# Loading W_down and wo at the end of a decode kernel: one queue for wo, and W_down split over partitions 96 + 11 + 11 + 10

## The chip, the cores and the metric

The kernel runs on one core of a Trainium2 chip. The metric is the device time of one execution in microseconds (us). The core has five engines with instruction streams of their own: TensorE (PE, matmuls, with its weight loads listed apart as PEld), VectorE (DVE), ScalarE (ACT), GpSimd (POOL) and SyncE (SP). SP and ACT can issue DMAs; 16 DMA engines carry them out, between HBM and the on-chip memory of 128 partitions.

## The reference

It is one step of decoding, of a gated mix of two branches for 4 tokens x of width 512:

```python
g = sigmoid((x * gate_w).sum(-1, keepdims=True))
a = attention(x @ wq, last 4096 keys and values of the caches) @ wo   # 32 heads on 8 KV heads
b = (relu(x @ W_gate) * (x @ W_up)) @ W_down                          # F = 1792
return g * a + (1 - g) * b
```

All data are bf16. wq is 512x4096, wo 4096x512, W_gate and W_up 512x1792, W_down 1792x512. Keys and values of the window are 4 tokens x 8 heads x 4096 x 128 each, so that the kernel reads 81 MB, of which 64 MiB are keys and values.

## The kernel before, in words

**Sets.** Attention is done in 8 sets (a token and half of its heads each). Set s loads 4 MB of keys into `Ksb` and 4 MB of values into `Vsb`; both have two halves, used in turn. PE transposes the keys (L353), ACT and DVE copy them back (L358, L360), PE makes the scores (L374), DVE adds the mask and takes the maximum (L384), ACT takes the exponential (L404), DVE transposes the probabilities (L414) and PE multiplies them with the values (L422, the function `values`).

**Order of the transfers.** Apart from x, gate_w and one piece of wo, all loads are issued by SP, one after the other, and SP waits in order: a load of keys waits for the scores of two sets before (L218), a load of values for the product of two sets before (L222). After the last keys come W_gate and W_up into the first half of `Ksb` (L231, L233), the values of the last set (L222), then W_down into the first half of `Vsb` (L236), which waits for `PV` of set 6, the last reader of that half, and then wo into `Wbig` (L241, L244), which waits for nothing but stands behind W_down's wait on SP.

**W_down and wo in memory.** Each is laid out with 128 partitions: a partition holds a contiguous piece of HBM, 14 tiles of 512 for W_down (14 KB) and 32 tiles of 512 for wo (32 KB). W_down is one DMA of 128 rows of 14 KB. wo comes in six pieces along the row: tiles 0 to 2 in a DMA that ACT issues (L499, `WOE`), tiles 3 to 15, 16 to 25 and 26 to 29 in three DMAs by SP (L241, `WO`), and tiles 30 and 31 in two, one for each half of the columns (L244, `WOL`).

**The end.** After the last set's maximum and exponential PE combines the heads of the first half (L441), makes gate and up (L458), waits for the last values, does `values(7)` (L422) and `combine(1)` (L441, L444), which yields `oq`. Then PE adds all of W_down's and wo's products into one accumulator (L508, the helper `product`): 28 matmuls with W_down, 6 with tiles 0 to 2 of wo, 26, 20 and 8 with the pieces of `WO`, and 2 for each half of the columns of `WOL`. As soon as a half of the columns is done, DVE (L525) or ACT (L526) copies it, and SP sends the result out (L547).

**Engine programs.** The class `Program` holds one list of operations per engine. `P.dma` gives a transfer a semaphore of its own that counts to 16 when it has landed; a wait is for a named event, and PE waits on the constant that the event has in `P.events`. An operation waits only for what its list of events says, and each engine works its list in order.

Of the kernel before, what the change touches and what calls it, by code (L numbers as in the profile page):

```python
# [19 lines left out]
NSET = 8  # L20
NFT = FF // 128
# [5 lines left out]
NTR = 2  # L27
NPAIR = 2
NFILL = 8
WO_EARLY = 3  # L30
WO_CUTS = (3, 16, 26, 30)
ACT_TAKES = (1, 3, 4, 6, 7)


# [105 lines left out]
def bass_gated_mix__sliding_block_cached__glu_gated_reglu__decode_kernel(  # L140
# [13 lines left out]
    with ExitStack() as ctx:  # L154
        def sb(name, shape, dt):
            return ctx.enter_context(nc.sbuf_tensor(name, shape, dt))

        Ksb = sb("Ksb", [128, 2, 16384], BF16)
        Vsb = sb("Vsb", [128, 2, 16384], BF16)
        Wbig = sb("Wbig", [128, 16384], BF16)  # L160
# [44 lines left out]
        Wo3 = Wbig[:, :].rearrange("p (i w) -> p i w", w=512)  # L205

        P = Program()
# [13 lines left out]
        def load_v(s):  # L221
            P.dma("sp", lambda e: e.dma_start(Vsb[:, s % 2, :], heads(A_v_cache, s)), ("V", s),  # L222
                  [("PV", s - 2)] if s >= 1 else [], sem=loop_sem("V", s))
# [4 lines left out]
        for s in range(1, NSET):  # L228
# [4 lines left out]
        P.dma("sp", lambda e: e.dma_start(Ksb[:, 0, 4 * FF:8 * FF], B_W_up.rearrange("(p t) f -> p (t f)", p=128)),  # L233
              ("WU",), [("SC", NSET - 2, NPAIR - 1)])
        load_v(NSET - 1)
        P.dma("sp", lambda e: e.dma_start(Vsb[:, 0, 0:NFT * 512], B_W_down.rearrange("(p i) w -> p (i w)", p=128)),  # L236
              ("WD",), [("PV", NSET - 2)])
        wo_src = A_wo.rearrange("(p i) w -> p (i w)", p=128)
        for k in range(len(WO_CUTS) - 1):
            lo, hi = 512 * WO_CUTS[k], 512 * WO_CUTS[k + 1]  # L240
            P.dma("sp", lambda e, lo=lo, hi=hi: e.dma_start(Wbig[:, lo:hi], wo_src[:, lo:hi]), ("WO", k))  # L241
        wo_src3 = A_wo.rearrange("(p i) w -> p i w", p=128)
        for u in range(2):
            P.dma("sp", lambda e, u=u: e.dma_start(Wo3[:, WO_CUTS[-1]:32, 256 * u:256 * u + 256],  # L244
                                                   wo_src3[:, WO_CUTS[-1]:32, 256 * u:256 * u + 256]), ("WOL", u))

# [170 lines left out]
        def values(s):  # L417
            par = s % 2
            for blk in range(64):
                g = blk % 4  # L420
                w = [("PTT", s), ("V", s), ("OSB", s - 1)] if blk == 0 else []
                P.op("pe", lambda e, g=g, blk=blk: e.matmul(  # L422
                    OB[32 * g:32 * g + 32, 0:256], pT[:, par, 32 * blk:32 * blk + 32],
                    Vsb[:, par, 256 * blk:256 * blk + 256],
                    start=(blk < 4), stop=(blk >= 60), tile_position=(0, 32 * g)),
                    ("PV", s) if blk == 63 else None, w)
            if s < 0:
                P.op("act", lambda e: e.copy(idle[:, 1:2], onesf[:, 0:1]),
                     ("OSB", s), [("ONESF",)], sem="va")
            else:  # L430
                P.op("act", lambda e: e.copy(osb[:, s, :], OB[:, 0:256]), ("OSB", s), [("PV", s)], sem="va")  # L431
# [22 lines left out]
        def gateup():  # L454
            for t in range(4):
                for which, W in ((0, Wg), (1, Wu)):
                    for g in range(4):
                        P.op("pe", lambda e, which=which, W=W, t=t, g=g: e.matmul(  # L458
                            TRT[32 * g:32 * g + 32, 512 * which:512 * which + FQ], xT[:, t, :], W[:, t, FQ * g:FQ * g + FQ],
                            start=(t == 0), stop=(t == 3), tile_position=(0, 32 * g)),  # L460
                            ("GU", which) if (t == 3 and g == 3) else None,
                            [("WG",), ("WU",)] + fills[-NTR:])
            G0 = TRT[:, 0:FQ]
            G1 = TRT[:, 512:512 + FQ]
            P.op("act", lambda e: e.activation(hrelu[:, :], G0, ACTF.Relu),
                 ("H0",), [("GU", 0)])
            P.op("dve", lambda e: e.tensor_tensor(
                hrow[:, :].rearrange("p (i c) -> p c i", i=NFT), G1.rearrange("p (c i) -> p c i", i=NFT),
                hrelu[:, :].rearrange("p (c i) -> p c i", i=NFT), ALU.mult), ("H1",), [("H0",), ("GU", 1)])
            P.op("dve", lambda e: e.transpose(hcol[:, :], hrow[:, :]), ("H2",), [("H1",)])  # L470
            P.op("dve", lambda e: e.tensor_tensor(
                hT[:, :].rearrange("p (i b) -> p i b", b=4),
                hcol[:, :].rearrange("p (i b) -> p i b", b=32)[:, :, 0:4],
                gsb[:, 4:8].rearrange("p (o b) -> p o b", o=1).to_broadcast([128, NFT, 4]), ALU.mult),
                ("H",), [("H2",), ("G",)], sem="vd")
# [19 lines left out]
        turn(NSET - 1)  # L495
        combine(0)
        gateup()
        early = 0
        P.dma("act", lambda e: e.dma_start(Wbig[:, 0:512 * WO_EARLY], wo_src[:, 0:512 * WO_EARLY]), ("WOE", 0), [], sem="wos")  # L499
        early = 16  # L500
        P.events[("WOE",)] = ("wos", early, None, 0)
        values(NSET - 1)
        combine(1)
        AB = SCT[:, 0:512]
        oq3 = oq[:, :].rearrange("p (b i) -> p b i", b=4)

        def product(stat, mov, u, start, stop, name, waits):
            P.op("pe", lambda e: e.matmul(AB[32 * u:32 * u + 4, 0:256], stat, mov[:, 256 * u:256 * u + 256],  # L508
                                          start=start, stop=stop, tile_position=(0, 32 * u)), name, waits)

        for i in range(NFT):
            for u in range(2):
                product(hT[:, 4 * i:4 * i + 4], Wd[:, i, :], u, i == 0, False, None,
                        [("WD",), ("H",), ("SCC", NSET - 1, 1)])
        for i in range(WO_EARLY):
            for u in range(2):
                product(oq3[:, :, i], Wo3[:, i, :], u, False, False, None, [("WOE",), ("OQ", 0), ("OQ", 1)])
        for k in range(len(WO_CUTS) - 1):
            for i in range(WO_CUTS[k], WO_CUTS[k + 1]):
                for u in range(2):  # L520
                    product(oq3[:, :, i], Wo3[:, i, :], u, False, False, None, [("WO", k)])
        for u in range(2):
            for i in range(WO_CUTS[-1], 32):
                product(oq3[:, :, i], Wo3[:, i, :], u, False, i == 31, ("ACC", u) if i == 31 else None, [("WOL", u)])
# [68 lines left out]
```

## Time and profile before

| | us |
|---|---|
| median of 3 runs | 196.21 |
| lowest and highest of these | 196.20 to 196.37 |
| the profiled execution's own time | 196.32 |
| its span, from the first to the last instruction | 195.1 |

The profiled execution lies 0.11 us above the median, and 1.2 us of its time lie outside its span. The profile lists each engine's busy time, the share of the 16 DMA engines that is busy in a stretch of time (1.00 is all 16), the chain of work that ended last, and groups of instructions by line. In a row of the timeline the columns are start, length, engine, line, operation, tiles, how many instructions were merged, and in brackets how long the engine was idle before and what released it.

### The profile page before, as it was taken

How to read it: one execution, taken by the hardware profiler on the slowest of the kernel's cores; microseconds unless marked ns; L12 is line 12 of the kernel's file. 1: busy time of each engine (PE TensorE's matmuls, PEld its weight loads, DVE VectorE, ACT ScalarE, POOL GpSimd, SP SyncE). 2: the span in 40 equal slices, each digit the busy share in tenths (PEclk: the TensorE clock that was granted, in tenths of full speed). 3: DMA queues.
4: the chain of work that ended last, by engine and by line, in shares of the span. 5: the costliest groups of instructions: out<-in, count | busy, mean ns of one | idle time of the engine just before them, and what ended most of it. 6: DMA issues, size and time to landing. Idle time of an engine off the chain costs nothing.

```text
span 195.1 us, 3497 instructions
## 1 busy us (share of the span) xinstructions
PE 129.0 (66%) x1578; PEld 101.0 (52%) x1578; DVE 73.8 (38%) x95; ACT 66.4 (34%) x77; POOL 11.6 (6%) x43
## 2 busy tenths in 40 slices
PE   0136398788669638861987298729964996732974
PEld 0112386576457427641965195519643974612752
DVE  0200054268239315820492039302931293280010
ACT  2005035465264453424243524352445244420000
POOL 8820000000000000000000000000000000000000
PEclk9999579999999999999799969975998599996699
DMA  6999999999999999999999999999999999999992
GB/s 216 437 437 437 437 437 433 430 433 430 430 433 443 437 437 430 430 430 430 432 430 432 430 430 430 430 430 430 430 430 430 430 401 432 456 430 391 418 408 73
DMA packets 4025, 81.11 MB, mean 416 GB/s; under 512 B 425, under 2 KB 946, under 8 KB 1202
## 3 DMA queue, kind: packets, MB, share of 16 engines
q1 hardware_dynamic: 3864, 80.61, 96.8%
q10 hardware_dynamic: 154, 0.40, 0.5%
q8 instruction: 5, 0.08, 0.2%
q14 instruction: 2, 0.02, 0.0%
HBM read 81.01 MB, written 0.00 MB: 415 GB/s over the span
## 4 chain that ended last, share of the span: by engine, by line
DMA 60%; PE 20%; DVE 14%; ACT 3%; issue 1%; SPq 1%
DMA Ksb<-in_A_k_cache_dram 48%; PE TRT L353 13%; DMA Wbig<-in_A_wo_dram 12%; DVE Ksb L360 7%; DVE pT L414 5%; PE SCT L374 3%; DVE sc L384 3%; ACT Ksb L358 3%; PE OB L422 2%; PE SCT L508 1%; SPq L241 0%; PE FB L391 0%; SPq L541 0%; ACT outr L526 0%; SPq L236 0%
## 5 line engine op out<-in xcount | busy, mean ns | idle before, releaser
L353 PE MATMUL TRT<-identw,Ksb 128*128 128x128 f32 x512 | 74.9, 306 | 27.1 <-DMA Ksb<-in_A_k_cache_dram 18.8
L353 PEld LDWEIGHTS TRT<-identw,Ksb 128*128 128x128 f32 x512 | 65.7, 158 | 37.3 <-DMA Ksb<-in_A_k_cache_dram 20.0
L358 ACT COPY Ksb<-TRT 128x1024 f32<-128x1024 f32 x40 | 40.5, 1012 | 59.6 <-PE TRT L353 59.5
L360 DVE COPY Ksb<-TRT 128x1024 f32<-128x1024 f32 x24 | 29.4, 1223 | 41.3 <-PE TRT L353 41.3
L422 PE MATMUL OB<-Vsb,pT 128*32 128x256 bf16 x576 | 18.9, 288 | 6.8 <-DMA Vsb<-in_A_v_cache_dram 6.8
L374 PE MATMUL SCT<-Ksb,qS 128*32 128x512 bf16 x256 | 16.9, 381 | 8.8 <-ACT Ksb L358 8.8
L422 PEld LDWEIGHTS OB<-Vsb,pT 128*32 128x32 bf16 x576 | 16.4, 102 | 9.7 <-issue 7.2
L384 DVE CUSTOM_DVE_ANT_0 sc<-SCT,mask,mx 128x1024 bf16<-128x1024 f32 x8 | 10.3, 1285 | 26.8 <-PE SCT L374 26.8
L404 ACT ACTIVATE sc<-sc,negmax 128x2048 bf16<-128x2048 bf16 x8 | 16.0, 2002 | 10.8 <-DVE negmax L396 10.8
L414 DVE STREAM_TRANSPOSE pT<-sc 128x2048 bf16<-128x2048 bf16 x8 | 18.4, 2302 | 2.2 <-ACT sc L404 2.2
L374 PEld LDWEIGHTS SCT<-Ksb,qS 128*32 128x32 bf16 x256 | 5.2, 94 | 15.7 <-ACT Ksb L358 11.4
L431 ACT COPY osb<-OB 128x256 f32<-128x256 f32 x8 | 3.0, 372 | 30.4 <-PE OB L422 30.4
L384 DVE CUSTOM_DVE_ANT_0 sc<-SCT,mask 128x1024 bf16<-128x1024 f32 x8 | 9.8, 1225 | 2.2 <-PE SCT L374 2.2
L341 POOL COPY qS<-qW 128x64 bf16<-128x64 bf16 x8 | 1.8, 237 | 112.6 <-PE SCT L374 104.5
L391 PE MATMUL FB<-identw,mx 128*128 128x128 f32 x18 | 4.4, 324 | 5.7 <-issue 5.7
L396 DVE CUSTOM_DVE_ANT_0 mrow<-FB,qmask 128x128 f32<-128x128 f32 x8 | 2.3, 291 | 12.8 <-PE FB L391 12.8
L391 PEld LDWEIGHTS FB<-identw,mx 128*128 128x128 f32 x18 | 2.7, 187 | 7.6 <-issue 7.6
L293 PE MATMUL FB<-identw,xw 5*128 5x5 f32 x4 | 0.6, 263 | 8.5 <-POOL m L268 8.5
L508 PE MATMUL SCT<-Wbig,oq 128*4 128x256 bf16 x64 | 4.4, 273 | 1.8 <-DMA Wbig<-in_A_wo_dram 1.8
L311 PE MATMUL SCT<-Vsb,xT 128*32 128x512 bf16 x32 | 3.6, 631 | 2.9 <-DMA Vsb<-in_A_wq_dram 2.9
L293 PEld LDWEIGHTS FB<-identw,xw 5*128 5x128 f32 x4 | 0.6, 206 | 8.5 <-DVE xw L287 8.5
L441 PE MATMUL TRT<-osb,Wsel 128*64 128x128 f32 x32 | 4.3, 292 | 0.5 <-ACT osb L431 0.5
(61 smaller groups left out, 41.7 us busy)
## 6 DMA issues: line engine op xcount, KB each, us to landing
Ksb<-in_A_k_cache_dram SPq DMA_DIRECT2D x8, 4096.0 KB, 25.0
Vsb<-in_A_v_cache_dram SPq DMA_DIRECT2D x8, 4096.0 KB, 32.9
Vsb<-in_A_wq_dram SPq DMA_DIRECT2D x1, 4096.0 KB, 12.3
Ksb<-in_B_W_gate_dram SPq DMA_DIRECT2D x1, 1792.0 KB, 18.9
Ksb<-in_B_W_up_dram SPq DMA_DIRECT2D x1, 1792.0 KB, 22.8
Vsb<-in_B_W_down_dram SPq DMA_DIRECT2D x1, 1792.0 KB, 16.9
Wbig<-in_A_wo_dram SPq DMA_DIRECT2D x1, 1664.0 KB, 20.5
Wbig<-in_A_wo_dram SPq DMA_DIRECT2D x1, 1280.0 KB, 23.1
```

Source lines behind the costliest of these rows:

```text
L311: P.op("pe", lambda e, half=half, t=t, g=g, col=col: e.matmul(SCT[32 * g:32 * g + 32, 512 * half:512 * half + 512], xT[:, t, :], Wq3[:, t, ...
L353: P.op("pe", lambda e, bk=bk, cc=cc, c=c: e.transpose(bk[:, cc * 128:(cc + 1) * 128], Kw[:, s % 2, c * 128:(c + 1) * 128], identw[:, :]), ...
L358: P.op("act", lambda e: e.copy(dst, bk), ("KTC", s, i), [("KT", s, i)], sem="va")
L360: P.op("dve", lambda e: e.tensor_copy(dst, bk), ("KTC", s, i), [("KT", s, i)], sem="vd")
L374: P.op("pe", lambda e, a=a, o=o, hb=hb, bank=bank: e.matmul(SCT[32 * a:32 * a + 32, 512 * hb:512 * hb + 512], qS[:, s % 2, o, :], k4[:, 16 ...
L384: P.op("dve", lambda e: e.tensor_tensor_reduce(sc[:, s % 2, pair * 1024:(pair + 1) * 1024], SCT[:, :], mask[:, :], 1.0, mx[:, s % 2, 0:1] ...
L391: P.op("pe", lambda e: e.matmul(FB[:, 384:512], mx[:, par, 1:2].to_broadcast([128, 128]), identw[:, :], start=True, stop=True), ("MT", s), ...
L404: P.op("act", lambda e: e.activation(sc[:, par, :], sc[:, par, :], ACTF.Exp, bias=negmax[:, par:par + 1], scale=SCALE, accum_out=rowsum[:, ...
L414: P.op("dve", lambda e: e.transpose(pT[:, par, :], sc[:, par, :]), ("PTT", s), [("EXP", s), ("PV", s - 2) if s >= 1 else None], sem="vd")
L422: P.op("pe", lambda e, g=g, blk=blk: e.matmul(OB[32 * g:32 * g + 32, 0:256], pT[:, par, 32 * blk:32 * blk + 32], Vsb[:, par, 256 * blk:256 ...
L441: P.op("pe", lambda e, k=k, lo=lo: e.matmul(CB[r, 0:128], Wsel[:, lo:lo + 64], ov[:, half, :, 32 * k:32 * k + 32], start=(k == 0), stop=(k ...
L508: P.op("pe", lambda e: e.matmul(AB[32 * u:32 * u + 4, 0:256], stat, mov[:, 256 * u:256 * u + 256], start=start, stop=stop, tile_position=( ...
```

## The change

All of wo is now issued by SP: the piece that ACT issued is gone, and SP's first piece of wo holds tiles 0 to 15 instead of 3 to 15. W_down, 128 rows before in one DMA, now comes in four: the first carries partitions 0 to 95, the other three carry partitions 96, 99, ... 126 (11 rows), 97, 100, ... 127 (11 rows) and 98, 101, ... 125 (10 rows). All four count on one semaphore, and PE waits until it has 64. The products with tiles 0 to 2 of wo now stand behind the landing of the first piece.

```diff
-WO_EARLY = 3
-WO_CUTS = (3, 16, 26, 30)
+WO_CUTS = (0, 16, 26, 30)
...
-        P.dma("sp", lambda e: e.dma_start(Vsb[:, 0, 0:NFT * 512], B_W_down.rearrange("(p i) w -> p (i w)", p=128)),
-              ("WD",), [("PV", NSET - 2)])
+        wd_src = B_W_down.rearrange("(p i) w -> p (i w)", p=128)
+        wd_parts = [slice(0, 96)] + [slice(96 + a, 96 + a + 3 * n - 2, 3) for a, n in ((0, 11), (1, 11), (2, 10))]
+        for k, part in enumerate(wd_parts):
+            P.dma("sp", lambda e, part=part: e.dma_start(Vsb[part, 0, 0:NFT * 512], wd_src[part, :]),
+                  ("WD", k), [("PV", NSET - 2)], sem="wd")
+        P.events[("WD",)] = ("wd", 16 * len(wd_parts), None, 0)
...
-        early = 0
-        P.dma("act", lambda e: e.dma_start(Wbig[:, 0:512 * WO_EARLY], wo_src[:, 0:512 * WO_EARLY]), ("WOE", 0), [], sem="wos")
-        early = 16
-        P.events[("WOE",)] = ("wos", early, None, 0)
...
-        for i in range(WO_EARLY):
-            for u in range(2):
-                product(oq3[:, :, i], Wo3[:, i, :], u, False, False, None, [("WOE",), ("OQ", 0), ("OQ", 1)])
...
-                    product(oq3[:, :, i], Wo3[:, i, :], u, False, False, None, [("WO", k)])
+                    product(oq3[:, :, i], Wo3[:, i, :], u, False, False, None, [("WO", k), ("OQ", 0), ("OQ", 1)])
```

## The prediction

> **What bounds the kernel now.** I read the page first (parts 1 to 3, then the DMA issues), then the chain in order of time, the timeline of the last 30 us, and then the busy share of the DMA engines in quarters of a microsecond at the end.
>
> ```profile
> PE 129.0 (66%) x1578; PEld 101.0 (52%) x1578; DVE 73.8 (38%) x95; ACT 66.4 (34%) x77; POOL 11.6 (6%) x43
> ...
> DMA  6999999999999999999999999999999999999992
> ...
> q1 hardware_dynamic: 3864, 80.61, 96.8%
> q10 hardware_dynamic: 154, 0.40, 0.5%
> q8 instruction: 5, 0.08, 0.2%
> ```
>
> No engine is busy for more than 66% of the span, while the 16 DMA engines are at 9 tenths or more from the second slice to the last but one. SP's queue (q1) alone takes 96.8% of their time. The kernel is bound by transfers, and what can move its time is when the last byte lands. How the chain ends says the same:
>
> ```profile
> 166.97 0.33 SPq L236
> 167.30 0.04 issue
> 167.34 0.43 SPq L241
> 167.77 0.04 issue
> 167.81 23.12 DMA Wbig<-in_A_wo_dram
> 190.94 0.04 issue
> 190.98 1.26 PE SCT L508 x20
> ```
>
> The transfers of wo are issued at 167 and land 23 us later, since they stand behind those in front of them. Now the end as the timeline has it:
>
> ```profile
> 185.53 1.69 PE L508 MATMUL SCT<-Vsb,hT 128*4 128x256 bf16 x28
> ...
> 187.06 0.49 PE L508 MATMUL SCT<-Wbig,oq 128*4 128x256 bf16 x6
> 187.88 1.30 PEld L508 LDWEIGHTS SCT<-Wbig,oq 128*4 128x4 bf16 x26 [0.62 <-DMA Wbig<-in_A_wo_dram]
> 187.89 1.59 PE L508 MATMUL SCT<-Wbig,oq 128*4 128x256 bf16 x26 [0.33 <-DMA Wbig<-in_A_wo_dram]
> ...
> 190.98 2.37 PE L508 MATMUL SCT<-Wbig,oq 128*4 128x256 bf16 x32 [1.51 <-DMA Wbig<-in_A_wo_dram]
> 192.24 0.53 PEld L508 LDWEIGHTS SCT<-Wbig,oq 128*4 128x4 bf16 x10 [0.29 <-DMA Wbig<-in_A_wo_dram]
> 192.96 0.10 PEld L508 LDWEIGHTS SCT<-Wbig,oq 128*4 128x4 bf16 x2 [0.19 <-DMA Wbig<-in_A_wo_dram]
> ```
>
> PE stands still four times in L508, each time until a piece of wo has landed (0.62, 1.51, 0.29 and 0.19 us by the brackets). A later landing is passed on in full to the end; an earlier one too, up to the sum of the last three waits, about 2 us.
>
> The last view decides this case. The column before the last is the busy share of the 16 DMA engines, so that share times 16 is how many are still at work:
>
> ```profile
> 190.50:190.75 0.25, 0.00 (x0) 0.00 (x0) 0.00 (x0) 0.00 (x0) 0.00 (x0) 1.00 0.85 283
> 190.75:191.00 0.25, 0.02 (x2) 0.02 (x4) 0.00 (x0) 0.00 (x0) 0.00 (x0) 1.00 0.47 152
> 191.00:191.25 0.25, 0.25 (x6) 0.21 (x8) 0.00 (x0) 0.00 (x0) 0.00 (x0) 1.00 0.42 150
> 191.25:191.50 0.25, 0.25 (x10) 0.21 (x6) 0.00 (x0) 0.00 (x0) 0.00 (x0) 1.00 0.33 109
> 191.50:191.75 0.25, 0.25 (x8) 0.20 (x6) 0.00 (x0) 0.00 (x0) 0.00 (x0) 1.00 0.31 100
> 191.75:192.00 0.25, 0.25 (x10) 0.18 (x4) 0.00 (x0) 0.00 (x0) 0.00 (x0) 1.00 0.26 78
> 192.00:192.25 0.25, 0.25 (x8) 0.01 (x2) 0.00 (x0) 0.00 (x0) 0.00 (x0) 1.00 0.48 111
> 192.25:192.50 0.25, 0.25 (x6) 0.21 (x8) 0.00 (x0) 0.00 (x0) 0.00 (x0) 1.00 0.11 31
> ```
>
> The 16 don't finish together. At 190.6 there are 0.85 x 16 = 14 at work, from 191.25 on five (0.33 x 16 = 5.3, 0.31 x 16 = 5.0), then four, and the last stop about 192.4 (part of the 0.48 is an instruction packet). So some eleven engines are done near 190.8, five are late, and the latest is 192.4 - 190.8 = 1.6 us behind. Had all finished together, it would have been some 1.1 us earlier: the shares from 190.50 on add up to 3.23 quarters, 0.81 us for each engine, which gives 191.3. Why five are late the views only suggest: q8's five instruction packets share the same engines, and at 0.2% of 16 engines' 195.1 us they take about 6 us together, over 1 us each. No view gives an engine's number.
>
> **The change part by part.**
>
> *W_down in four DMAs.* This alone can move the end. Its price per row comes from the issue rows and the rate while it lands:
>
> ```profile
> Vsb<-in_B_W_down_dram SPq DMA_DIRECT2D x1, 1792.0 KB, 16.9
> ```
>
> ```profile
> 179.00:183.40 4.40, 3.81 (x65) 2.94 (x66) 0.00 (x0) 0.37 (x1) 0.00 (x0) 0.50 1.03 431
> ```
>
> 1792 KB over 128 partitions is 14 KB (14336 B) a row, and 431 GB/s over 16 engines is 26.9 GB/s each: 0.53 us a row. Before, an engine had 128 / 16 = 8 rows, 4.3 us. How few rows are dealt out can be read from q10: ACT's queue carried the 128 rows of the early piece of wo with 16 completions, x with 4 rows and gate_w with 1; its 154 packets are 128 + 16 + 4 + 4 + 1 + 1, so that a DMA of 4 rows ends with 4 completions, one for each engine it used. A DMA of 11 rows, by the same reading, uses 11 engines, one row each. If the three short ones begin at the same engine, ten engines get 6 + 3 = 9 rows, one gets 8 and five get 6.
>
> [...]
>
> What a row costs in the 96-row DMA the trace does not show, as every big load in it fills 128 partitions. Bounds: at best 0.53 us, so 6 rows are 3.2 us. At worst the DMA takes as long as one of 128 rows, for each partition still receives 14 KB: 8 row times, 4.3 us. The nearest row is the W_down load itself, same bytes per partition, and I take its time, the worse end. Then ten engines spend 8 + 3 = 11 row times where they had 8: 3 x 0.53 = 1.6 us more. The better end is one row, 0.5 us more.
>
> Which of the late engines are among the ten? Five late ones in 16 put about three there. I take one that finishes in the middle of the late group, about 191.8, where the share falls from 0.31 to 0.26: 191.8 + 1.6 = 193.4 against 192.4 now, **1.0 us later**. If only early finishers were among the ten, 190.8 + 1.6 = 192.4, nothing; if the latest is, the full 1.6 us.
>
> *The issue of these.* SP issues three DMAs more. An issue takes 0.33 to 0.47 us (rows below), so wo's last one goes out about 1.4 us later, at 171 instead of 169.7. The engines are then still at work on the last values: PE waits for them until 179.11. That cover of 8 us makes it free; without it, it would cost the 1.4 us.
>
> ```profile
> 166.97 0.33 SPq L236 DMA_DIRECT2D Vsb<-in_B_W_down_dram  x1
> ...
> 167.34 1.39 SPq L241 DMA_DIRECT2D Wbig<-in_A_wo_dram  x3
> ...
> 168.77 0.95 SPq L244 DMA_DIRECT2D Wbig<-in_A_wo_dram  x2
> ...
> 172.15 0.36 ACTq L499 DMA_DIRECT2D Wbig<-in_A_wo_dram  x1
> ...
> 179.11 3.61 PE L422 MATMUL OB<-Vsb,pT 128*32 128x256 bf16 x64 [6.83 <-DMA Vsb<-in_A_v_cache_dram]
> 182.77 0.37 ACT L431 COPY osb<-OB 128x256 f32<-128x256 f32 x1 [10.08 <-PE OB L422]
> ```
>
> *PE's wait for W_down.* It landed 16.9 us after 166.97, at 183.9, and PE first needs it at 185.53: 1.6 us of cover. The early piece of wo (384 KB, 0.9 us at 431 GB/s) no longer mixes with it, which brings it forward; the dealing may put it back by 1.6 us. Net about 184.6, free. Behind that wait stand only L508's products, which wait for wo anyhow.
>
> *wo on one queue.* The same bytes, so nothing at the end. ACT saves 0.36 us at 172.15, but then it was idle 10.08 us up to 182.77: nothing. The six matmuls with tiles 0 to 2 (0.49 us) no longer run before the first piece of SP lands but behind it: 26 become 32, which at 1.59 / 26 a piece adds 0.37 us to a stretch followed by a wait of 1.51 us. Hidden; without that wait it would cost the 0.37. One row per partition is not cut in two any more; that can save at most some hundredth of a microsecond per row, I take nothing, with -0.1 us as its end.
>
> **Sum.** +1.0 us on the profiled 196.32 gives 197.3; that execution lies 0.11 us above the median of 196.21, so the forecast for the median is **197.2 us**.
>
> **The rivals.**
>
> *A, even shares, no loss in the 96-row DMA.* The ten engines get one row more, 0.53 us, and at least one of the latest is among them: 196.21 + 0.53 = 196.7. For it: each engine moves its 26.9 GB/s whether its neighbours are early or late, so each may well have a rate of its own. Against: all those loads reach all 128 partitions. Chance 0.25.
>
> *B, the other sign: the spared engines are the late ones.* Then the last two or three lose two rows, 1.07 us, and the end is set by whoever is next. From the point on where the latest engine (192.4) is among the five with 6 rows, and the 96-row DMA costs its six rows only, the kernel is faster. If all five late ones are spared: 192.4 - 1.07 = 191.35, and the eleven reach 190.8 + 0.53 = 191.3, so 1.0 us is gained, 195.2. If late ones that finish about 191.5 are among the ten, they end at 192.0: 0.3 to 0.4 us, 195.8. For it: the number of late engines, five, is that of the spared ones. Against: nothing ties the late engines to neighbouring numbers; five at random are seldom all spared. I put it at 195.8, chance 0.20.
>
> *C, the short DMAs don't begin at the same engine.* Then the rows are dealt 8 each again and nothing changes: 196.2. For it speaks nothing in the views, against it nothing either. Chance 0.10.
>
> The forecast, that writing to 96 partitions is slower per row, has 0.45, of which a tenth may lie over 198.3 (all eleven rows on the latest engine, and short rows that collide with wo's).
>
> [...]
>
> **How the numbers follow.** A measurement of this kernel can tell about 0.2%, 0.39 us. Faster by more than that (below 195.8): half of B and a little, 0.13. Slower by more (above 196.6): the forecast except its mildest tenth, 0.41, and three quarters of A, 0.19, together 0.60. Within: 0.27. The range for 8 in 10 reaches from B's price, 195.8, to the forecast with the latest engine hit and half a microsecond of collisions, 196.2 + 1.6 + 0.5 = 198.3; about 0.1 is left out on each side.
>
> **What would show it.** In the quarters at the end: by the forecast the share falls to a few engines about 191 as now, but the last stop near 193.4. By A the same with the end near 192.9. By B the tail is short and high, ended before 192.1. By C the rows look like those above. The landing of W_down should be the second sign: about 184.6 by the forecast, 183 to 183.5 by A and B. If PE's wait before the 28 matmuls grew, or its four waits in L508 vanished, the cover that I counted on would be wrong. The forecast fails if the 96-row DMA runs at full rate, which the rate between 179 and 183 would show: 431 GB/s still, instead of some 300.

## The result, and the profile after

The changed kernel takes 203.55 us (median of 4 runs, 201.92 to 204.18) against 196.25 us before: a ratio of 1.036 with a 95% interval of 1.033 to 1.039, 7.3 us slower. The sign was forecast (chance 0.60), the size was not: 197.2 us was predicted, 198.3 us was the end of the range. The profiled execution of the changed kernel took 203.17 us, its span 201.9 us.

Parts 1 to 3 of its page; the third line is the busy share of the DMA engines in 40 slices, the fourth what they moved:

```profile
PE 131.9 (65%) x1578; PEld 103.6 (51%) x1578; DVE 73.8 (37%) x95; ACT 66.4 (33%) x77; POOL 11.5 (6%) x43
...
DMA  6999999999999999999999999999999999999991
GB/s 222 494 422 415 422 415 432 480 425 415 422 412 435 467 441 415 422 415 417 474 435 430 422 415 422 428 474 428 428 415 422 410 459 448 392 216 208 322 373 54
...
q1 hardware_dynamic: 3896, 81.01, 97.0%
```

The third line looks as before: the engines are busy to the end. The fourth does not. Two slices of 5 us near the end move 216 and 208 GB/s. Stretches from 166 us on, first of the kernel before, then of the changed one (columns: stretch, its length, then PE, PEld, DVE, ACT and POOL, PE's clock, busy share of the DMA engines, GB/s):

```profile
166.00:176.00 10.00, 4.99 (x88) 3.63 (x76) 5.31 (x11) 3.01 (x4) 0.00 (x0) 1.00 1.02 437
176.00:180.00 4.00, 0.89 (x20) 0.80 (x24) 0.00 (x0) 0.00 (x0) 0.00 (x0) 0.65 0.98 411
180.00:184.00 4.00, 3.53 (x56) 2.75 (x49) 0.00 (x0) 0.37 (x1) 0.00 (x0) 0.50 1.01 421
184.00:188.00 4.00, 3.67 (x53) 3.03 (x52) 0.64 (x3) 0.00 (x0) 0.00 (x0) 1.00 0.97 412
188.00:192.00 4.00, 2.49 (x46) 1.81 (x42) 0.00 (x0) 0.00 (x0) 0.00 (x0) 1.00 0.78 294
```

```profile
166.00:176.00 10.00, 4.59 (x72) 3.24 (x64) 4.92 (x11) 3.01 (x4) 0.00 (x0) 1.00 1.03 441
176.00:180.00 4.00, 0.00 (x0) 0.00 (x0) 0.00 (x0) 0.00 (x0) 0.00 (x0) 0.50 0.99 229
180.00:184.00 4.00, 3.36 (x66) 2.70 (x67) 0.00 (x0) 0.37 (x1) 0.00 (x0) 0.65 1.06 229
184.00:188.00 4.00, 1.85 (x18) 1.76 (x17) 0.64 (x3) 0.00 (x0) 0.00 (x0) 1.00 0.98 189
188.00:192.00 4.00, 1.92 (x20) 1.18 (x22) 0.00 (x0) 0.00 (x0) 0.00 (x0) 0.70 0.94 364
```

Up to 176 us the two are alike. Then, for the 12 us in which the end of the last values, W_down and the front of wo land, all 16 engines are as busy as ever (0.98 to 1.06) and move half as much. Busy at half the rate means that each row takes about twice as long (W_down's 1.04 us against 0.54, below). From 176 to 188 us it moved 4 x (229 + 229 + 189) = 2588 KB, the kernel before 4 x (411 + 421 + 412) = 4976 KB (in thousands of bytes): 2388 KB less, which at some 415 GB/s is 5.8 us. The rest is in the tail:

```profile
196.00:196.50 0.50, 0.50 (x14) 0.32 (x8) 0.00 (x0) 0.00 (x0) 0.00 (x0) 1.00 0.77 294
196.50:197.00 0.50, 0.17 (x4) 0.00 (x0) 0.00 (x0) 0.00 (x0) 0.00 (x0) 1.00 0.74 256
197.00:197.50 0.50, 0.00 (x0) 0.00 (x0) 0.00 (x0) 0.00 (x0) 0.00 (x0) 1.00 0.59 201
197.50:198.00 0.50, 0.11 (x3) 0.10 (x5) 0.00 (x0) 0.00 (x0) 0.00 (x0) 1.00 0.29 102
198.00:198.50 0.50, 0.50 (x12) 0.42 (x10) 0.00 (x0) 0.00 (x0) 0.00 (x0) 1.00 0.25 80
198.50:199.00 0.50, 0.50 (x12) 0.30 (x8) 0.00 (x0) 0.00 (x0) 0.00 (x0) 1.00 0.12 36
199.00:199.50 0.50, 0.50 (x12) 0.32 (x9) 0.00 (x0) 0.00 (x0) 0.00 (x0) 1.00 0.16 45
```

These shares add up to 2.92 halves, 1.46 us for each engine, so with all finishing together the end of the transfers would be at 197.5. The last packet of wo ends at 199.3: 1.8 us lost to unequal finishes, where the kernel before lost 1.1. With 5.8 that makes 6.5 of the 6.85 us between the two profiled executions.

The traces also hold a record of every DMA packet, one for each row of these loads, and it shows which rows are slow. W_down's 128 rows took 0.54 us each before. In the changed kernel they average 1.04 us: 0.99 for the first 96 to start, 1.20 for the rest. And it is not W_down alone: four rows of the last values, in front of it, took 1.67 to 2.28 us instead of 1.22, and 54 of the 128 rows of wo's first piece, behind it, up to 1.60 us instead of 0.61. Spread over 16 engines the excess is 0.2 us in the values, 4.0 in W_down and 2.1 in wo, together 6.3 us.

What became of PE's waits is in the timeline:

```profile
166.57 2.94 SPq L238 DMA_DIRECT2D Vsb<-in_B_W_down_dram  x4
...
180.17 3.19 PE L425 MATMUL OB<-Vsb,pT 128*32 128x256 bf16 x64 [8.28 <-DMA Vsb<-in_A_v_cache_dram]
...
190.09 3.11 PE L507 MATMUL SCT<-Vsb,hT 128*4 128x256 bf16 x28 [4.23 <-DMA Vsb<-in_B_W_down_dram]
...
194.75 1.92 PE L507 MATMUL SCT<-Wbig,oq 128*4 128x256 bf16 x32 [1.56 <-DMA Wbig<-in_A_wo_dram]
197.89 2.31 PE L507 MATMUL SCT<-Wbig,oq 128*4 128x256 bf16 x32 [1.22 <-DMA Wbig<-in_A_wo_dram]
```

W_down, which was to land 1.6 us ahead of its use, is now 4.23 us late, and PE still waits for wo afterwards.

### The profile page after: what moved, and what is told of

It reads as the page before. It is cut to its first block, busy times and chain, and to the rows that moved or that the text cites. A ratio compares the mean times of both kernels' runs of the same rounds, so it can differ in the third digit from the quotient of the medians.

```text
span 201.9 us, 3499 instructions
## 1 busy us (share of the span) xinstructions
PE 131.9 (65%) x1578; PEld 103.6 (51%) x1578; DVE 73.8 (37%) x95; ACT 66.4 (33%) x77; POOL 11.5 (6%) x43
## 4 chain that ended last, share of the span: by engine, by line
DMA 60%; PE 20%; DVE 13%; ACT 3%; SPq 2%; issue 1%
DMA Ksb<-in_A_k_cache_dram 46%; PE TRT L356 14%; DMA Wbig<-in_A_wo_dram 14%; DVE Ksb L363 6%; DVE pT L417 4%; PE SCT L377 3%; DVE sc L387 3%; ACT Ksb L361 3%; PE OB L425 2%; SPq L238 1%; PE SCT L507 1%; SPq L244 0%; PE FB L394 0%; SPq L537 0%; ACT outr L522 0%
## 5 line engine op out<-in xcount | busy, mean ns | idle before, releaser
L356 PE MATMUL TRT<-identw,Ksb 128*128 128x128 f32 x512 | 76.8, 312 | 24.2 <-DMA Ksb<-in_A_k_cache_dram 16.2
L356 PEld LDWEIGHTS TRT<-identw,Ksb 128*128 128x128 f32 x512 | 68.1, 162 | 34.0 <-DMA Ksb<-in_A_k_cache_dram 17.5
L507 PE MATMUL SCT<-Vsb,hT 128*4 128x256 bf16 x28 | 3.1, 413 | 4.2 <-DMA Vsb<-in_B_W_down_dram 4.2
```

The lines of the kernel that those rows point to most:

```text
L356: P.op("pe", lambda e, bk=bk, cc=cc, c=c: e.transpose(bk[:, cc * 128:(cc + 1) * 128], Kw[:, s % 2, c * 128:(c + 1) * 128], identw[:, :]), ...
```

## The experiments

The theory after the result: the loss is in the four DMAs of W_down, and it comes from which partitions a DMA writes (P). Rivals: wo's queue; the unequal shares and the short DMAs (E, later S); the reading side in HBM (H); the mere number of DMAs. The edits are shown shortened, against the changed kernel. e3 to e8, e11, e12 and e15 are one execution each; as those of the changed kernel lie up to 2.3 us apart (201.92 to 204.18), smaller differences among slow versions say little.

**e1, wo's part alone.** W_down in one DMA as before, wo as in the change.

```diff
-        wd_parts = [slice(0, 96)] + [...]   # four DMAs
+        P.dma("sp", lambda e: e.dma_start(Vsb[:, 0, 0:NFT * 512], B_W_down...), ("WD",), [("PV", NSET - 2)])
```

> The change's wo part alone: wo's loads all on SP's queue, W_down in one DMA of 128 rows as before. If wo's queue has nothing to do with the loss (the theory I start from), 196.2 us within 0.3, and the rate between 176 and 189 us stays near 430 GB/s. The rival that ACT's early piece of wo had kept the DMA engines evenly filled gives the larger part of the 7 us here, some 200 us or more.

Measured: 196.21 us against 196.25, ratio 0.9997 (0.9988 to 1.0007). wo's part costs and brings nothing.

**e2, W_down's part alone.** The split, with ACT's early piece of wo kept.

```diff
+WO_EARLY = 3
+WO_CUTS = (3, 16, 26, 30)                  # and ACT's DMA of tiles 0 to 2, as before
```

> The change's W_down part alone: four DMAs over 96, 11, 11 and 10 rows, the first three tiles of wo issued by ACT as before. If the split makes the loss, about 203 us, with about 210 GB/s for ten microseconds after the last values have landed. If both parts are needed, clearly less, below 200 us.

Measured: 203.35 us, ratio 1.036 (1.0345 to 1.0379). The split makes all of the loss.

**e3, 96 and 32 rows.** By the prediction's reading of q10 no engine is spared any more.

```diff
-        wd_parts = [slice(0, 96)] + [... 11, 11 and 10 rows]
+        wd_parts = [slice(0, 96), slice(96, 128)]
```

> As the changed kernel, but W_down in two DMAs, partitions 0 to 95 and 96 to 127, so that every DMA engine carries 6 + 2 = 8 rows and none is spared. Theory P (two groups of partitions, 0 to 63 and 64 to 127, each taken at no more than half the full rate): 64 rows at half rate 4.3 us, then 32 at half 2.1, then the other 32 at half 2.1, 8.6 us where the one DMA needs 4.3, so 196.2 + 4.3 = 200.5 us. Theory E (the short DMAs on eleven engines make the loss, by unequal shares and by colliding with what the spared engines go on to): 196.2 us, at full rate.

Measured: 202.53 us. Theory E falls for most of the loss: with shares even by that reading, 6.3 of the 7.3 us are still there. P has the right side, and falls short by 2 us.

**e4, 64 and 64 rows.**

```diff
+        wd_parts = [slice(0, 64), slice(64, 128)]
```

> As the changed kernel, but W_down in two DMAs, partitions 0 to 63 and 64 to 127, 4 + 4 rows for every engine. Theory P: both at half rate, 8.6 us instead of 4.3, 200.5 us, with packets of 14 KB that take about 1.07 us instead of 0.54. Theory E: 196.2 us. A theory H, that the reading side in HBM makes it (which rows are read at the same time), can give either and is told apart by the next runs.

Measured: 202.89 us. Shares even by the same reading, again slow; P's 200.5 is too low again. Stretches of its profile:

```profile
176.00:180.00 4.00, 0.00 (x0) 0.00 (x0) 0.00 (x0) 0.00 (x0) 0.00 (x0) 0.50 1.14 198
180.00:184.00 4.00, 2.54 (x50) 2.23 (x53) 0.00 (x0) 0.00 (x0) 0.00 (x0) 0.50 0.87 194
184.00:188.00 4.00, 2.77 (x38) 2.37 (x30) 0.64 (x3) 0.37 (x1) 0.00 (x0) 0.97 1.07 231
```

P's working let the half rate end with W_down's 1835 KB. It lasts 12 us and 2492 KB, so that other rows are slowed as well. The packets agree: W_down's rows average 1.15 us, near P's 1.07, but 42 of the 128 rows of wo's first piece are slow too (up to 1.23 us instead of 0.61), and four rows of the last values.

**e5 to e7, the same two DMAs with other partitions or other rows.** e5 takes the even and the odd partitions, on both sides. e6 writes the halves 0 to 63 and 64 to 127 but reads the even and the odd rows; e7 writes even and odd partitions and reads the halves.

```diff
+        wd_parts = [(slice(0, 128, 2), slice(0, 128, 2)), (slice(1, 128, 2), slice(1, 128, 2))]   # e5: partitions, rows
+        wd_parts = [(slice(0, 64), slice(0, 128, 2)), (slice(64, 128), slice(1, 128, 2))]         # e6
+        wd_parts = [(slice(0, 128, 2), slice(0, 64)), (slice(1, 128, 2), slice(64, 128))]         # e7
```

> As the run with 64 + 64 rows, but the two DMAs carry the even and the odd partitions, read from the even and the odd rows of W_down. Theory P (a group of partitions has a rate of its own, the halves 0 to 63 and 64 to 127 at least): both DMAs reach all of the chip's memory, 196.2 us. Theory M (only a DMA of all 128 partitions gives every engine partitions of its own; with any other number of rows the engines fall on each other): about 202.5 us again.

> Two DMAs to partitions 0 to 63 and 64 to 127, read from the even and from the odd rows of W_down, so that W_down's rows stand on other partitions than its product expects. Theory P and M, by which the writing side makes the loss: 202.9 us, as with 64 + 64. Theory H (which rows of HBM are read at a time): as the run with even and odd rows.

> Two DMAs to the even and to the odd partitions, read from rows 0 to 63 and 64 to 127 of W_down, so that its rows stand on other partitions than the product expects. Theory P: as the run with even and odd rows, 196.2 us. Theory H: 202.9 us, as with 64 + 64. Theory M: about 202.5 us.

Measured beside 196.32 us of the kernel before: e5 195.97, e6 202.32, e7 196.25 us. With the destination in halves the kernel is slow whichever rows are read, with even and odd partitions it is fast whichever rows are read. H falls, and so does M in the form given there: 64 rows in a DMA can be as fast as 128. The same stretch of e5:

```profile
176.00:180.00 4.00, 1.56 (x32) 1.35 (x36) 0.00 (x0) 0.00 (x0) 0.00 (x0) 0.50 0.99 419
180.00:184.00 4.00, 3.52 (x56) 3.00 (x49) 0.00 (x0) 0.37 (x1) 0.00 (x0) 0.82 1.02 429
```

**e8, two DMAs of 128 partitions and half of the columns.**

```diff
+        for k, (lo, hi) in enumerate(((0, 3584), (3584, 7168))):
+            P.dma("sp", lambda e, lo=lo, hi=hi: e.dma_start(Vsb[:, 0, lo:hi], wd_src[:, lo:hi]), ("WD", k), ...)
```

> Two DMAs as well, but each over all 128 partitions with half of the columns (7 KB a row). All three theories: 196.2 us at full rate. If it is slow too, it is the number of DMAs or their size, and not the partitions, that makes the loss.

Measured: 196.1 us. It isn't the number of DMAs or their size.

**e9, the change's shares on spread partitions.**

```diff
+        wd_parts = [slice(0, 128, 2), slice(1, 128, 4), slice(3, 124, 12), slice(7, 128, 12), slice(11, 120, 12)]
```

> The change's shares without its partitions: 96 rows in two DMAs (the 64 even partitions, and 1, 5, ... 125), and the other 32 (3, 7, ... 127) in three DMAs of 11, 11 and 10 rows, twelve partitions apart. Engines carry 9, 8 or 6 rows as in the change, but every DMA is spread over all of the memory. By theory P the 7 us are gone. What is left is what the shares do: 195.2 to 195.8 us if the five spared engines are the late ones, 196.7 us if a late one is among the ten that get a row more, 196.2 us if rows are dealt out evenly after all. If the short DMAs made the loss, it stays near 203 us.

Measured: 199.43 us, ratio 1.0157 (1.0140 to 1.0174), outside all three numbers. Of the 7.3 us 4.1 are gone. The first two stretches show where the rest lies:

```profile
176.00:180.00 4.00, 1.50 (x32) 1.32 (x36) 0.00 (x0) 0.00 (x0) 0.00 (x0) 0.50 1.05 411
180.00:184.00 4.00, 3.52 (x54) 2.98 (x47) 0.00 (x0) 0.37 (x1) 0.00 (x0) 0.79 0.96 224
```

The 96 spread rows land at 411 GB/s; then, with the three short DMAs, the rate halves. They carry a quarter of W_down and cost 3.2 us, though they are spread. That is followed up in e13 to e15.

**e10, even and odd once more, in 11 executions.** The same code as e5.

> The run with the even and the odd partitions again (one look gave 195.97 us beside 196.32 us of the kernel before), in more rounds. The shares are 4 + 4 rows, so by all theories 196.2 us, no difference to before; a gain of 0.2 us or more would mean that the order in which rows are written matters too.

Measured: 196.24 us against 196.23, ratio 0.9999 (0.9990 to 1.0008). The 0.35 us of e5's single execution was chance.

**e11 and e12, how fine the groups are.** Eight DMAs of 16 partitions with a step of 8, and four of 32 with a step of 4.

```diff
+        wd_parts = [slice(a, 128, 8) for a in range(8)]     # e11
+        wd_parts = [slice(a, 128, 4) for a in range(4)]     # e12
```

> W_down in eight DMAs of 16 rows, partitions 0, 8, ... 120, then 1, 9, ... 121, and so on: one row for every engine in each DMA, each DMA reaching from end to end of the memory. If the only groups are the halves 0 to 63 and 64 to 127, 196.2 us. [...]

> W_down in four DMAs of 32 rows, partitions 0, 4, ... 124, then 1, 5, ... 125, and so on. [...] It is the control for the run with steps of 8: many small DMAs with strided partitions. If it is slow as well, strides or the number of rows make it and not the groups.

Measured: e11 203.03, e12 196.21 us. Steps of 8 reach from end to end and are as slow as the halves (202.89 us in e4); steps of 4 cost nothing against the 196.23 us of the kernel before. Groups that are just the two halves don't explain this, as by them e11 takes 196.2 us. If the partitions form groups, 0, 8, ... 120 fall on only a part of them; which partitions belong together no run shows. First e11, then e12:

```profile
176.00:180.00 4.00, 0.00 (x0) 0.00 (x0) 0.00 (x0) 0.00 (x0) 0.00 (x0) 0.50 1.07 193
180.00:184.00 4.00, 1.93 (x40) 1.66 (x44) 0.00 (x0) 0.00 (x0) 0.00 (x0) 0.50 0.97 208
```

```profile
176.00:180.00 4.00, 1.31 (x28) 1.15 (x32) 0.00 (x0) 0.00 (x0) 0.00 (x0) 0.52 0.98 416
180.00:184.00 4.00, 3.53 (x54) 2.77 (x47) 0.00 (x0) 0.37 (x1) 0.00 (x0) 0.62 1.00 420
```

**e13 to e15, shares or collisions.** W_down in one DMA again, behind it three DMAs of 8 rows into columns that nobody reads; only the partitions differ: steps of 4 in e13, steps of 12 in e14, neighbours in e15.

```diff
+        for k, part in enumerate([slice(a, a + 29, 4) for a in (0, 1, 2)]):        # e13
+        for k, part in enumerate([slice(a, a + 85, 12) for a in (3, 7, 11)]):      # e14
+        for k, part in enumerate([slice(a, a + 8) for a in (0, 8, 16)]):           # e15
+            P.dma("sp", lambda e, part=part: e.dma_start(Vsb[part, 0, NFT * 512:2 * NFT * 512], wd_src[part, :]), ...)
```

> W_down in one DMA of 128 rows, wo on SP's queue (196.2 us), and behind W_down three DMAs of 8 of its rows more, into columns of the value buffer that nobody reads: 24 rows extra, 3 for each of eight engines, partitions 0, 4, ... 28, then one and two further. By the step of 4 each engine writes, by theory K, the group of partitions that is its own in a DMA of 128 rows. Theory K (rows collide when two engines write one group): no collision, only 3 x 0.53 = 1.6 us more work on eight engines, so between 196.2 and 197.8 us. Theory S (unequal shares make the loss): the same number as in the next two runs.

> [...] Theory K: 1 to 3 us over the run with steps of 4, with 14 KB packets of about 1 us. Theory S: the same as there.

> [...] Theory K: the worst of the three, four engines in each group, so each row takes about four times 0.53 us and the kernel 3 to 6 us more than with steps of 4. Theory S: the same as there.

Measured: e13 197.59 us, ratio 1.0061 (1.0045 to 1.0078); e14 199.48 us, 1.0141 (1.0106 to 1.0176); e15 201.44 us. Same bytes, same number of rows, and 1.4, 3.3 and 5.2 us over e1's 196.2 (1.2, 3.1 and 5.1 over the 196.36 us of the kernel before that ran beside them). Theory S asked for one number and falls. K gave 196.2 to 197.8 for e13 and the order of the three, and e14 and e15 lie 1.9 and 3.9 us over e13, inside what it asked. The stretch in which the extra rows land, 180 to 184 us, for e13, e14 and e15:

```profile
180.00:184.00 4.00, 3.53 (x56) 2.78 (x46) 0.00 (x0) 0.37 (x1) 0.00 (x0) 0.74 1.01 424
```

```profile
180.00:184.00 4.00, 3.53 (x51) 2.85 (x44) 0.00 (x0) 0.37 (x1) 0.00 (x0) 0.62 1.02 290
```

```profile
180.00:184.00 4.00, 3.53 (x50) 2.85 (x40) 0.00 (x0) 0.37 (x1) 0.00 (x0) 0.50 1.13 293
```

At much the same busy share 424, 290 and 293 GB/s. The 24 extra rows of e13, by the reading of q10 three on each of eight engines and by K without a collision, cost 1.2 to 1.4 us, somewhat less than 3 x 0.53; those of e14 and e15 cost more than twice that. That rows of several engines meet on a group there is the author's estimate: the runs show the times and rates, and no view a group. In e13 none of the 152 rows of 14 KB took more than 0.55 us, though its short DMAs have only 8 rows each; so it isn't the few rows in a DMA that make e11 slow.

K's total for e15 came out, its working did not: it asked for rows of four times 0.53 us, 2.1 us, and the slowest of the 152 took 1.35. No run shows its four engines in a group. Most of the excess lies in the rows of wo behind, which K did not price (per engine 1.6 of 2.5 us in e15, 1.3 of 1.9 in e14). That e15 fell inside its span is in part luck.

No version beat the kernel before: the best, e1, e8, e10 and e12, equal it.

## Why the prediction was wrong, point by point

*What bounds the kernel* held: transfers, to the last microsecond; each delay was passed on (PE's waits for landings behind the values: 4.23, 1.56 and 1.22 us).

*wo on one queue* held: nothing, shown by e1.

*The price of a row in the 96-row DMA* is the step that failed. The prediction bounded it by 0.53 us (6 rows in 3.2 us) and by "as long as one of 128 rows", 4.3 us, and took the latter. That was no upper bound: at the measured 0.99 us a row, 6 rows are 5.9 us. The rate that was to fall from 431 to some 300 GB/s fell to 229. The sign came from this step and is no luck, but the reason given for it was another. It reasoned about how much each partition receives, as if the partitions were filled one beside the other whatever DMA fills them. e4 to e7 and e11 show what counts instead: which partitions the rows in flight write. In the three stretches from 176 to 188 us the halves (e4, e6) and the steps of 8 (e11) go at 193 to 238 GB/s, the even and odd partitions (e5, e7) at 404 to 429. e4's three are 198, 194 and 231: the rate stays down while both halves land. That groups of partitions, each with a rate of its own, are behind this is the author's estimate. Rows of wo behind them and of the values before them were slowed too, 2.3 us of excess per engine, and the sum had no term for that: in it the harm is W_down's own rows.

*The shares* were mis-sized as well. That three more rows on an engine cost about 1.6 us was about right (1.2 to 1.4 in e13), but e9's short DMAs, with the 96 rows healed, cost 3.2 us. That they meet rows of other engines there was estimated, not shown. The prediction named such collisions, as half a microsecond at the end of its range.

*Issue*: the four DMAs took SP 2.94 us instead of 4 x 0.33 to 0.47, and were hidden as said (PE's last values came only at 180.17).

*PE's wait for W_down*: 1.6 us of cover were counted against at most 1.6 us of delay; PE waited 4.23 us there. It cost nothing by itself, as wo was later still.

*The rivals*: A, B and C all went without a loss in the 96-row DMA; its 0.99 us a row excludes that, and so do e3's 6.3 us of loss with shares that by the prediction's reading are even. The slower 96-row DMA had the largest chance, 0.45, but its price was taken from a load of 128 rows, where a row took 0.54 us.

*What stays open.* Which engine writes which row of a DMA no view shows, so the 12 us of half rate were not rebuilt row by row. That wo's rows are slowed its packets show; that this comes from meeting W_down's rows on one group is argued from e14 and e15, not shown by itself. Whether the engines spared by the change were the late ones stayed hidden behind the half rate.

## What to carry to other kernels

A busy DMA engine is no proof of a fast one (here 229 GB/s at a share of 0.99, where the kernel before had 411 at 0.98): read the GB/s beside the share, and where the share stays at 1.0 while the rate halves, ask which partitions the DMAs in flight write. Try a split of a load along its columns (here 196.1 us) or by a step of 2 or 4 partitions (196.24 and 196.21) before one into blocks of partitions (202.53 and 202.89); and before you even out the ends of DMA engines by hand, measure three extra rows on spread and on neighbouring partitions (here 1.4 and 5.2 us). A bound for an operation that the trace does not show is only a bound if the row it is taken from would have shown the resource that the new form crowds.

## What the runs showed of the hardware that was not expected

Two DMAs of 64 rows differ by 6.65 us in a kernel of 196 (202.89 against 196.24 us) by the choice of partitions alone. Eight DMAs of 16 rows from end to end of the memory (203.03 us) are as slow as two of its halves. And 24 rows of 14 KB, 0.8 us of traffic at 430 GB/s, cost 1.4, 3.3 or 5.2 us by where they land.
